# Weighing the 47-point groups three times as heavily in the table that paces spectral steps beside channel mixing

## The chip, the core and the metric

The kernel runs on one core of one Trainium2 chip. The metric is the device time of one execution in microseconds (us); lower is better. The time before is 2440.4 us, the median of three runs (2438.03 to 2441.76). On the core, TensorE (PE) does the matrix products, VectorE (DVE), ScalarE (ACT) and GpSimd (POOL) do elementwise work, and SyncE (SP) and ACT issue the transfers (DMA). Each engine works through its own queue in the order in which the program was built.

## The reference

Eight images of 3008 tokens by 256 channels go through two blocks in fp32.

```python
X = np.fft.rfft(x, axis=1)                       # along the tokens
Yr = Xr @ w_r - Xi @ w_i + b_r
Yi = Xr @ w_i + Xi @ w_r + b_i
Y  = soft-threshold of Yr and Yi by 0.01
x  = np.fft.irfft(Y, n=3008, axis=1)             # first block's output

h  = relu(x.transpose(0, 2, 1) @ w_tok1) @ w_tok2   # mixing over tokens
u  = x + h.transpose(0, 2, 1)
out = u + relu(u @ w_ch1) @ w_ch2                   # mixing over channels, 256 -> 1536 -> 256
```

## The kernel before, in words

**Units.** The images are worked in five units: image 0, image 1, and the pairs (2, 3), (4, 5) and (6, 7). They are called units 0 to 4 here. A product in near-fp32 accuracy is made of three matrix products of a high and a low part (helper `mm3`, lines 196 to 198), so one fp32 product shows as three rows.

**Spectral part of a unit** (generator `spectral`). Since 3008 = 47 x 64, the Fourier transform is done in two stages.

- *The 47-point groups* (`dft47`): 13 groups a unit, each of 5 values of the second index. For one group a tile `x` is loaded from memory three groups ahead, its sum and difference `sd` are formed (line 247 on POOL, line 248 on DVE; unit 1 has both on DVE), and split into a high part `xh` (ACT, line 146) and a low part `xl` (DVE, line 149). Six matrix products make the two results `p` (three for each). ACT copies them to a tile `a` (line 269), and ACT's queue then issues the store of `a` to the scratch tensor `a_d` (line 271). The tile `a` has two buffers.
- *The mixing steps*: 12 steps for each image of the unit. A step loads a slice of `a_d`, transforms it (64-point products `px`, line 469), copies it (`xf` by ACT, line 471), adds two of its parts (`xf` by POOL, line 472), splits it (`xth` on ACT, `xtl` on DVE), multiplies by the mixing weights (18 matrix products `pm`, lines 196 to 198), adds the bias and soft-thresholds on DVE (`z`, lines 498 and after), splits to `yh` and `yl`, and then does the first stage of the inverse transform (`pi`, copied to `bt` and stored to `b_d`) and the first token product (`gp`).

**Channel part of a unit** (generator `channel`). The unit's tokens are cut into chunks of up to 512. For each chunk the program forms the token mixing and the last stage of the inverse transform (`pu`), the first channel product (`ph`, six matrix products for each of 12 slices, rectified to `hh` on ACT and `hlo` on DVE), and the second (`po`, six for each slice). For units 2 to 4 the channel part runs after all spectral work is over, by Strassen's scheme (`channel7`).

**What sets the order.** The spectral parts of units 1 and 2 are woven between the channel slices of unit 0, and those of units 3 and 4 between the channel slices of unit 1 (table `BESIDE`). The last loop of `tile_kernel` does this with two budgets in estimated microseconds. `left_c` is the channel work still to come; every channel slice yields its estimate, which is taken off. `left_s` is the spectral work still to come; every spectral step yields its estimate, which is taken off in the same way. After each channel slice, spectral steps are written out until `left_s` is no more than `pace * left_c`, where `pace` was set to `left_s / left_c`. So a spectral step with a larger estimate is followed by more channel work. Where a generator yields "wait" (before a unit's first group where POOL forms `sd`, and after its last one), 10 us of channel work pass with no spectral step, and `pace` is set anew. A list scheduler then sees the written order and may move neighbouring instructions.

The estimate of a 47-point group is `0.7 * w / C`: 0.7 us for an image alone (w = 256, C = 256), 1.4 us for a pair. A mixing step's pieces yield 0.9, 2.15, 0.68 and 1.37 us per image. Over an image that sums to 13 x 0.7 + 12 x 5.1 = 70.3 us, the number in `left_s`.

Of the kernel before, what the change touches and what calls it, by code (L numbers as in the profile page):

```python
# [17 lines left out]
B, N, C = 8, 3008, 256  # L18
# [5 lines left out]
UNITS = [[0], [1]] + [[2 * p, 2 * p + 1] for p in range(1, NP)]  # L24
NG = 13
# [11 lines left out]
SEVEN = (2, 3, 4)  # L37
SPILL = (1, 2, 3, 4)
CW7 = 2 * CW
BESIDE = {0: [1, 2], 1: [3, 4]}  # L40


# [84 lines left out]
def tile_kernel(ctx: ExitStack, tc: tile.TileContext, io):  # L127
# [115 lines left out]
    def sum_diff(x, g, w, eng, pool):  # L243
        if eng is None:
            return x
        sd = t4([120, 2, w], "sd") if pool is None else wk.tile([120, 2, w], F32, tag=("xtl", "xf", "wt", "et")[g % 4], name="sd", bufs=2)
        eng.tensor_tensor(out=sd[:, 0], in0=x[:, 0], in1=x[:, 1], op=ALU.add)
        V.tensor_tensor(out=sd[:, 1], in0=x[:, 0], in1=x[:, 1], op=ALU.subtract)
        return sd

    def split_x(sd, w):
        xh, xl = hl([120, 2, w], "xh"), hl([120, 2, w], "xl")
        split(xh, xl, sd, S, V)
        return xh, xl

    def stage1(sd, dst, g, w, pool):
        n = GS if g < NG - 1 else N2 - GS * (NG - 1)
        a = ev([120, 2, w], "a") if pool is None else pool.tile([120, 2, w], F32, name="a", bufs=4)
        each = 512 // w
        for i0 in range(0, 2, each):  # L260
            pt = bank("p1")
            for i in range(i0, i0 + each):
                o = (i - i0) * w
                if pool is None:
                    mm3(pt[:, o:o + w], f1r[:, 0, i], f1r[:, 1, i], sd[0][:, i], sd[1][:, i], True, True)
                else:
                    PE.matmul(pt[:120, o:o + w], lhsT=f1[:, i], rhs=sd[:, 0], start=True, stop=False)
                    PE.matmul(pt[:120, o:o + w], lhsT=f1[:, 2 * i], rhs=sd[:, 1], start=False, stop=True)
            S.copy(out=a[:, i0:i0 + each].rearrange("p i w -> p (i w)"), in_=pt[:120])
        rows = dst.rearrange("(i n) k w -> (n k) i w", i=2)  # L270
        PUT.dma_start(out=rows[g * 120:g * 120 + n * KH, :, :w], in_=a[:n * KH])


    def stage1_turned(sd, z, g):
        n = GS if g < NG - 1 else N2 - GS * (NG - 1)
        pt = bank("p1")
        for t in range(2):
            for i in range(2):
                o = (2 * t + i) * GS * KH
                PE.matmul(pt[:, o:o + GS * KH], lhsT=sd[:, i, t * 128:(t + 1) * 128], rhs=f1[:, i], start=True, stop=True)  # L280
        S.copy(
            out=z.rearrange("p k (q n) -> p q k n", q=4)[:, :, :, g * GS:g * GS + n],
            in_=pt[:, :4 * GS * KH].rearrange("p (q n k) -> p q k n", q=4, n=GS)[:, :, :, :n],
        )

    def dft47(load, dst, w, ahead, eng, pool=None, turned=False):
        xs = [load(g) for g in range(ahead)]
        yield "wait" if eng is G else 0.0
        sds = {}

        def prepare(g):
            if g < NG:
                sds[g] = sum_diff(xs[g], g, w, eng, pool)
                xs[g] = None

        def divide(g):
            if g < NG and pool is None:
                sds[g] = split_x(sds[g], w)

        prepare(0)  # L300
        prepare(1)
        divide(0)
        for g in range(NG):
            if g + ahead < NG:
                xs.append(load(g + ahead))
            prepare(g + 2)
            divide(g + 1)
            if turned:
                stage1_turned(sds.pop(g), dst, g)
            else:  # L310
                stage1(sds.pop(g), dst, g, w, pool)
            yield 0.7 * w / C

    def f2cols(k1):
        j0 = (15 * k1) % N2
# [11 lines left out]
    def prepare_w1(pool, after):  # L327
        def load(g):
            f = load_wide(None, 2 * DT, pool, ("hl", "o")[g % 7 % 2], raw=raws.pop(g), after=after.get(g)).rearrange("p (i w) -> p i w", i=2)
            load_raw1()  # L330
            return f

        return dft47(load, a_w, DT, 2, None, pool)
# [222 lines left out]
    def spectral(u):  # L556
        p = parts(u)
        nb = p.nb
        yield from dft47(p.load_unit, p.a, p.w, 3, V if u == 1 else G)
        yield "wait"  # L560
        steps = [(kp, b) for kp in range(KP) for b in range(nb)]
# [42 lines left out]
    def begin(sp):  # L604
# [14 lines left out]
        with tc.tile_pool(name="early", bufs=1) as early:  # L619
# [3 lines left out]
            wc["fw"] = early.tile([128, 2, 128], F32, name="fw")  # L623
            z = wc["z"] = const.tile([128, KH, 2 * 128], F32, tag="w1", name="z")
            x = dft47(p.load_unit, z, p.w, NG, V, early, True)
            DMA.dma_start(out=wc["eye"], in_=io["eye"])
            next(x)
# [81 lines left out]
    for u, bs in enumerate(UNITS):  # L709
        total, at = N * len(bs), 0  # L710
        step = CW7 if u in SEVEN else CW
        widths = [k * TOKS for k in sizes] if u == 0 else [total % step] + [step] * (total // step)
# [47 lines left out]
    def make_u(g):  # L760
# [6 lines left out]
        for m in homes:  # L767
            if m not in ufs:
                ufs[m] = wc["uf"].tile([128, 2, CW7 if chunks[m][0] in SEVEN else CW], F32, name="uf", bufs=3)
        for ct in range(2):  # L770
# [230 lines left out]
    def channel7(ns):  # L1001
        channels.close()
        wc["tail"] = ctx.enter_context(tc.tile_pool(name="tail", bufs=1, reuse_waits="tile"))
        behind = None
        half = NF // 2
        for n in ns:
            after = n + 1 if n + 1 < len(chunks) else None
            mine = list(needs[after]) if after else []
            for p in range(half):
                hs = first7(n, p)  # L1010
                if behind:
                    second7(*behind, 0, (0, 1))
                if p < len(mine):
                    make_u(mine[p])
                    if p + 1 < len(mine):
                        load_wt2(mine[p + 1])
                        load_b2(mine[p + 1])
                if p == half - 2:
                    load_ahead(n + 2)
                if behind:  # L1020
                    second7(*behind, 1, (0, 1))
                    if p == 0:
                        for k in range(2):
                            finish7(behind[0], k, 2)
                behind = n, p, hs
                if after and p == half - 2:
                    sum_u(after)
                    for i in range(2):
                        split_u7(after, i)
                if after and p == half - 1:  # L1030
                    for i in range(2, 7):
                        split_u7(after, i)
        for k in range(2):
            for f in range(2):
                second7(*behind, f, (k,))
            finish7(behind[0], k, 2 - k)

    def run(gen):
        for _ in gen:
            pass  # L1040
# [3 lines left out]
    done = begin(sp)  # L1044
    for n, (u, at, cw) in enumerate(chunks):
        if u in SEVEN:
            channel7(range(n, len(chunks)))
            break
        if at == 0:
            if u:  # L1050
                sp, done = chain.from_iterable(spectral(v) for v in BESIDE[u]), 0.0
            else:
                sp = chain(sp, *(spectral(v) for v in BESIDE[u][1:]))
            left_s = sum(len(UNITS[v]) for v in BESIDE[u]) * 70.3 - done
            mine = [w for cu, _, w in chunks if cu == u]
            made = sum(k for gu, _, _, k in groups if gu == u) - sizes[0]
            left_c = 32.7 * (sum(mine) - mine[-1]) / CW + 3.6 * made * TOKS / GW + 0.5
            pace, hold = 0.0, left_c - (25.0 if u == 0 else 0.0)
        for c in channel(n):
            if c == "end":  # L1060
                run(sp)
                left_s = -1e9
                continue
            left_c -= c
            if hold is not None:
                if left_c > hold:
                    continue
                pace, hold = left_s / left_c, None
            while left_s > pace * left_c:
                step = next(sp, None)  # L1070
                if step is None:
                    left_s = -1e9
                elif step == "wait":
                    hold = left_c - 10.0
                    break
                else:
                    left_s -= step
# [36 lines left out]
```

## Time and profile before

| What | Value | Where it is from |
| --- | --- | --- |
| Median of three runs | 2440.4 us | times |
| The profiled execution's own time | 2437.33 us | times |
| Its span, first to last instruction | 2435.5 us | page, first line |
| PE busy | 2379.9 us (98% of the span) | page, part 1 |
| DVE, ACT, POOL busy | 1442.1, 1176.7, 309.1 us | page, part 1 |
| Mean granted TensorE clock | 0.994 | spans and clocks |
| Spectral parts of units 1 to 4 beside channel work | about 182 to 1130 us of the span | the tiles' first and last instructions |

The profile's busy shares are of one execution. A view by windows gives each engine's busy time in a stretch of the span, with PEclk, the share of its full speed that TensorE's clock was granted there, and the share of time that the 16 DMA engines worked. A view of waits names for an engine's idle time the instruction that ended it: "PE p L197 <- DVE xl L149" is idle time of PE before a product into `p` on line 197, ended by the DVE instruction on line 149 that writes `xl`. In a timeline, "[2.94 <-DMA a_d<-a]" behind a row means 2.94 us of idle time before it, ended by the landing of a store to `a_d`.

### The profile page before, as it was taken

What the parts mean: (1) busy time and instruction counts of PE and PEld (TensorE: products, weight loads), DVE (VectorE), ACT (ScalarE), POOL (GpSimd) and SP (SyncE); (2) the same over time, 40 slices, a digit from 0 to 9 for tenths busy, and PEclk for the clock granted to TensorE, in tenths of its full rate; (3) what the DMA queues carried; (4) which work ended last, traced back from release to release, by engine and by line L of the source; (5) the groups of instructions that cost most, each with busy time, mean ns of one, the idle gap of its engine ahead of it and who ended that gap; (6) DMA issues with size and microseconds to landing.
All of it is one profiled execution on the core that took longest, in us unless ns stands there. A gap on an engine that the chain in (4) does not pass through costs nothing.

```text
span 2435.5 us, 32450 instructions
## 1 busy us (share of the span) xinstructions
PE 2379.9 (98%) x12524; PEld 2063.7 (85%) x12524; DVE 1442.1 (59%) x2256; ACT 1176.7 (48%) x2105; POOL 309.1 (13%) x259
## 2 busy tenths in 40 slices
PE   8999999999999998999999999999999999999999
PEld 7778887989878886888988888898888889888887
DVE  7986666665455555655565555556555555555564
ACT  6764455444344445443454444444444544444443
POOL 0001333333123333331000000000000000000000
PEclk9999999999999999999999999999999999999999
DMA  8864465335453357333312102221211222122100
GB/s 215 250 211 140 137 192 177 123 122 168 136 164 105 104 155 214 104 113 100 95 59 66 61 21 77 66 80 59 66 61 36 62 66 80 59 66 63 53 2 35
DMA packets 146312, 253.48 MB, mean 104 GB/s; under 512 B 10549, under 2 KB 98701, under 8 KB 146157
## 3 DMA queue, kind: packets, MB, share of 16 engines
q1 hardware_dynamic: 115225, 194.24, 26.7%
q10 hardware_dynamic: 30932, 57.16, 7.1%
q8 instruction: 99, 1.62, 0.3%
q14 instruction: 56, 0.46, 0.1%
HBM read 163.41 MB, written 87.95 MB: 103 GB/s over the span
## 4 chain that ended last, share of the span: by engine, by line
PE 84%; DMA 6%; DVE 4%; ACT 3%; issue 2%; POOL 1%; SPq 1%; ACTq 0%; DVEq 0%; POOLq 0%
PE po L196 10%; PE po L198 10%; PE po L197 10%; PE pu L776 5%; DMA a_d<-a 3%; PE sx L196 3%; PE sx L198 3%; PE sx L197 3%; PE ph L196 2%; PE ph L197 2%; PE ph L198 2%; PE px L469 2%; PE sw L196 2%; PE sw L198 2%; PE sw L197 2%; PE pu L196 2%
## 5 line engine op out<-in xcount | busy, mean ns | idle before, releaser
L196 PE MATMUL po<-hh,w2h 128*128 128x512 f32 (+3 forms) x1176 | 453.0, 385 | 0.0
L197 PE MATMUL po<-hlo,w2h 128*128 128x512 f32 (+3 forms) x1176 | 449.5, 382 | 1.4 <-DVE hlo L815 1.4
L198 PE MATMUL po<-hh,w2l 128*128 128x512 f32 (+3 forms) x1176 | 448.7, 382 | 0.0
L944 ACT ACTIVATE hh<-sn 128x512 fp32r<-128x512 f32 (+1 forms) x432 | 270.8, 627 | 86.3 <-DVE sn L964 56.7
L945 DVE SCALAR_TENSOR_TENSOR hlo<-sn,hh 128x512 fp32r<-128x512 f32 (+1 forms) x432 | 290.3, 672 | 10.1 <-ACT hh L944 0.6
L197 PEld LDWEIGHTS po<-hlo,w2h 128*128 128x128 f32 x1176 | 220.9, 188 | 41.1 <-DVE hlo L815 4.5
L198 PEld LDWEIGHTS po<-hh,w2l 128*128 128x128 f32 x1176 | 220.8, 188 | 38.3
L196 PEld LDWEIGHTS po<-hh,w2h 128*128 128x128 f32 x1176 | 221.0, 188 | 37.8 <-ACT hh L814 1.4
L953 DVE TENSOR_TENSOR sn<-sq,sn 128x512 f32<-128x512 f32 (+1 forms) x108 | 73.4, 679 | 290.2 <-PE sq L198 267.0
L949 ACT COPY sn<-sx 128x512 f32<-128x512 f32 (+1 forms) x108 | 62.5, 579 | 341.7 <-PE sx L198 341.6
L815 DVE SCALAR_TENSOR_TENSOR hlo<-ph,hh 128x512 fp32r<-128x512 f32 (+3 forms) x156 | 98.9, 636 | 98.5 <-ACT hh L814 98.2
L196 PE MATMUL pm<-wmh,xth 128*128 128x256 f32 x504 | 148.0, 294 | 5.1 <-ACT xth L146 2.8
L198 PE MATMUL pm<-wmh,xtl 128*128 128x256 f32 x504 | 143.0, 285 | 3.0 <-DVE xtl L149 2.7
L197 PE MATMUL pm<-wml,xth 128*128 128x256 f32 x504 | 142.1, 282 | 0.0
L783 ACT COPY uf<-pu 128x470 f32<-128x470 f32 (+15 forms) x152 | 60.5, 426 | 167.8 <-PE pu L776 167.0
L149 DVE TENSOR_TENSOR xtl<-xf,xth 128x768 fp32r<-128x768 f32 x84 | 80.8, 962 | 100.2 <-ACT xth L146 100.2
L814 ACT ACTIVATE hh<-ph 128x512 fp32r<-128x512 f32 (+3 forms) x156 | 86.7, 556 | 105.3 <-PE ph L198 101.2
L776 PEld LDWEIGHTS pu<-g,b 96*128 96x128 f32 x1024 | 130.9, 191 | 3.4
L776 PE MATMUL pu<-g,b 96*128 96x94 f32 x1024 | 129.2, 271 | 0.0
L149 POOL TENSOR_TENSOR yl<-z,yh 128x512 fp32r<-128x512 f32 x72 | 97.0, 1347 | 220.1 <-ACT yh L146 212.8
L196 PE MATMUL ph<-uh,w 128*128 128x512 f32 (+3 forms) x312 | 120.5, 387 | 1.9 <-DVE z L498 1.0
L146 ACT CAST xth<-xf 128x768 fp32r<-128x768 f32 x84 | 70.1, 835 | 102.0 <-POOL xf L472 101.9
(185 smaller groups left out, 5395.3 us busy)
## 6 DMA issues: line engine op xcount, KB each, us to landing
wt<-wt_d SPq DMA_DIRECT2D x28, 940.0 KB, 5.8
x<-in_x SPq DMA_DIRECT2D x39, 480.0 KB, 5.1
a<-a_d SPq DMA_DIRECT2D x36, 512.0 KB, 3.8
b_d<-bt ACTq DMA_DIRECT2D x36, 512.0 KB, 3.3
a_d<-a ACTq DMA_DIRECT2D x36, 480.0 KB, 4.9
wt<-wt_d SPq DMA_DIRECT2D x21, 752.0 KB, 5.1
b<-b_d SPq DMA_DIRECT2D x32, 480.0 KB, 6.4
out<-uf SPq DMA_DIRECT2D x26, 512.0 KB, 4.5
```

What stands on the lines that cost most here:

```text
L146: S.copy(out=hi, in_=src)
L149: lo_eng.tensor_tensor(out=lo, in0=src, in1=hi.bitcast(F32), op=ALU.subtract)
L196: PE.matmul(out, lhsT=wh, rhs=xh, start=start, stop=False, skip_group_check=more)
L197: PE.matmul(out, lhsT=wh, rhs=xl, start=False, stop=False, skip_group_check=more)
L198: PE.matmul(out, lhsT=wl, rhs=xh, start=False, stop=stop, skip_group_check=more)
L776: PE.matmul(pt[:, s * TOKS:(s + 1) * TOKS], lhsT=b2[:, s, cs], rhs=g2[:, 0 if s0 + s == 0 else 1], start=False, stop=s == k - 1)
L814: S.activation(out=hh, in_=pt, func=AF.Relu)
L815: V.scalar_tensor_tensor(out=hlo, in0=pt, scalar=0.0, in1=hh.bitcast(F32), op0=ALU.max, op1=ALU.subtract)
L944: S.activation(out=hh, in_=t, func=AF.Relu)
L945: V.scalar_tensor_tensor(out=hlo, in0=t, scalar=0.0, in1=hh.bitcast(F32), op0=ALU.max, op1=ALU.subtract)
L949: S.copy(out=snap[0], in_=x)
L953: V.tensor_tensor(out=snap[0], in0=q, in1=snap[0], op=ALU.add)
```

## The change

A constant `SLOW = 2.1` takes the place of 0.7 in what a 47-point group yields, where the group runs beside channel work; the groups that run elsewhere (the weights' and unit 0's, which are given a pool) keep 0.7. The sum in `left_s` is raised by what that adds: 13 x 1.4 = 18.2 us an image, so 88.5 in place of 70.3. No product, copy or transfer is added or taken away. Units 2 to 4 keep Strassen's scheme (`SEVEN` is as it was).

```diff
@@ -37,6 +37,7 @@
 SEVEN = (2, 3, 4)
 SPILL = (1, 2, 3, 4)
 CW7 = 2 * CW
+SLOW = 2.1
 BESIDE = {0: [1, 2], 1: [3, 4]}
@@ -309,7 +310,7 @@
                 stage1_turned(sds.pop(g), dst, g)
             else:
                 stage1(sds.pop(g), dst, g, w, pool)
-            yield 0.7 * w / C
+            yield (SLOW if pool is None else 0.7) * w / C
@@ -1051,7 +1052,7 @@
                 sp, done = chain.from_iterable(spectral(v) for v in BESIDE[u]), 0.0
             else:
                 sp = chain(sp, *(spectral(v) for v in BESIDE[u][1:]))
-            left_s = sum(len(UNITS[v]) * 70.3 for v in BESIDE[u]) - done
+            left_s = sum(len(UNITS[v]) * (70.3 + NG * (SLOW - 0.7)) for v in BESIDE[u]) - done
```

The added line moves every later line number by one: line 269 before is line 270 after.

How this moves instructions is seen at two places. The first is ACT's queue at the first groups of unit 3 (images 4 and 5). `COPY a` moves a group's result out of `p` (two copies for a group, in two buffers `a`), `DMA a_d` issues its store, `CAST xh` splits the input of a later group, and `ACTIVATE hh` belongs to one channel slice. Before:

```order
L269 COPY a<-p_6251 120x512
L269 COPY a<-p_6256 120x512
L814 ACTIVATE hh<-ph 128x448
L271 DMA a_d_91<-a 120x2x512
L146 CAST xh<-sd 120x1024
L269 COPY a<-p_6289 120x512
L269 COPY a<-p_6294 120x512
L146 CAST xh<-sd 120x1024
L271 DMA a_d_91<-a 120x2x512
L269 COPY a<-p_6310 120x512
L269 COPY a<-p_6315 120x512
```

With the change, from the same group of the unit on:

```order
L270 COPY a<-p_6268 120x512
L270 COPY a<-p_6273 120x512
L815 ACTIVATE hh<-ph 128x448
L272 DMA a_d_91<-a 120x2x512
L147 CAST xh<-sd 120x1024
L270 COPY a<-p_6306 120x512
L270 COPY a<-p_6311 120x512
L815 ACTIVATE hh<-ph 128x448
L272 DMA a_d_91<-a 120x2x512
L147 CAST xh<-sd 120x1024
L270 COPY a<-p_6344 120x512
```

Before, groups follow each other with no channel slice between some of them; with the change a channel slice (`hh`) stands between each two of these groups. Over a unit, from the first product of its groups to the last, the PE rows of channel work (`ph`, `po`, and `pu` in brackets) go from 27 to 58 for the last ten groups of unit 1, from 60 to 124 (0 to 20) for unit 2, from 54 to 96 (22 and 22) for unit 3, and from 36 to 72 (0 to 20) for unit 4. Further on in unit 3 (the sixth to eighth group) three groups still stand with none between them.

The second place is PE's queue at an early mixing step of unit 3. `px` makes a step's 64-point products; the `pm` rows behind it are those of the step before it or of the step itself. Before:

```order
L197 MATMUL pm_6798<-wml,xth 128x256
L198 MATMUL pm_6798<-wmh,xtl 128x256
L469 MATMUL px<-f_78,a_6715 128x128 x4
L196 MATMUL ph<-uh,w_961 128x512
L197 MATMUL ph<-ul,w_961 128x512
L198 MATMUL ph<-uh,w_961 128x512
```

With the change, at the like step:

```order
L198 MATMUL pm_6866<-wml,xth 128x256
L199 MATMUL pm_6866<-wmh,xtl 128x256
L470 MATMUL px<-f_78,a_6783 128x128 x4
L197 MATMUL pm_6906<-wmh,xth 128x256
L198 MATMUL pm_6906<-wml,xth 128x256
L199 MATMUL pm_6906<-wmh,xtl 128x256
```

Before, a channel slice (`ph`, then `po`) stood between the `px` rows and the next step's `pm`; with the change it does not. Call a step bare if no more than the 18 `pm` products of another step and four `px` products stand between its `px` and its own `pm`. Leaving each unit's first step aside, 17 steps are bare with the change (1, 3, 4 and 9 in units 1 to 4) and 8 before (0, 0, 1 and 7). On every engine the number of instructions of each kind is the same in both programs.

More of the change, by code (lines that the diff above doesn't have):

```diff
@@ L1053, in tile_kernel @@
                 sp = chain(sp, *(spectral(v) for v in BESIDE[u][1:]))
-            left_s = sum(len(UNITS[v]) for v in BESIDE[u]) * 70.3 - done
+            left_s = sum(len(UNITS[v]) * (70.3 + NG * (SLOW - 0.7)) for v in BESIDE[u]) - done
             mine = [w for cu, _, w in chunks if cu == u]
```

## The prediction

> **What bounds the kernel now.** I read the page first, then busy time by windows, then the waits of the worst windows, then ACT's timeline there. The page:
>
> ```profile
> span 2435.5 us, 32450 instructions
> PE 2379.9 (98%) x12524; PEld 2063.7 (85%) x12524; DVE 1442.1 (59%) x2256; ACT 1176.7 (48%) x2105; POOL 309.1 (13%) x259
> ```
>
> TensorE (PE) is the bound, idle for 2435.5 - 2379.9 = 55.6 us in all. The change neither adds nor removes a product, so it can win only such idle time and time at a lowered clock. Where these lie shows when the span is cut at the 47-point groups of units 1 to 4 (rows 1, 3, 5 and 7) and the mixing steps behind each (rows 2, 4, 6 and 8); the last row is Strassen's part, which holds its place:
>
> ```profile
> core 0: us, PE busy (x) PEld busy (x) DVE busy (x) ACT busy (x) POOL busy (x), PEclk, DMA share, GB/s
> 180.00:208.00 28.00, 23.96 (x123) 20.63 (x123) 17.51 (x35) 14.43 (x27) 0.00 (x0) 0.88 0.64 187
> 208.00:348.00 140.00, 135.30 (x875) 125.41 (x874) 87.23 (x131) 63.90 (x116) 49.07 (x40) 0.99 0.46 138
> 348.00:388.00 40.00, 34.89 (x143) 25.34 (x142) 31.24 (x40) 27.31 (x44) 15.91 (x9) 1.00 0.80 249
> 388.00:652.00 264.00, 256.77 (x1583) 240.48 (x1581) 147.14 (x232) 112.01 (x203) 73.80 (x64) 0.99 0.41 126
> 652.00:690.00 38.00, 31.98 (x133) 24.19 (x133) 25.63 (x24) 23.31 (x38) 16.15 (x9) 0.96 0.83 249
> 690.00:911.00 221.00, 220.21 (x1295) 195.31 (x1294) 124.44 (x180) 98.36 (x170) 71.84 (x64) 1.00 0.41 126
> 911.00:949.00 38.00, 32.40 (x114) 21.56 (x113) 23.96 (x22) 24.16 (x38) 16.11 (x9) 0.91 0.78 230
> 949.00:1135.00 186.00, 182.05 (x1112) 162.14 (x1111) 108.30 (x158) 83.70 (x143) 63.48 (x58) 1.00 0.34 113
> 1135.00:2436.00 1301.00, 1296.09 (x6249) 1109.07 (x6247) 726.27 (x1127) 611.26 (x1116) 0.00 (x0) 1.00 0.20 60
> ```
>
> The four short stretches hold 144 us and PE's idle time in them is 4.0 + 5.1 + 6.0 + 5.6 = 20.7 us. The clock adds to that: a stretch of 28 us at a mean clock of 0.88 has lost 0.12 x 28 = 3.4 us. The others lost 0, 0.04 x 38 = 1.5 and 0.09 x 38 = 3.4 us. Together the units lose 7.4, 5.1, 7.5 and 9.0, that is 29.0 us. The mixing steps, 811 us long, have 4.7 + 7.2 + 0.8 + 4.0 = 16.7 us of idle time.
>
> What PE waits for in the groups of unit 4, by the waits of window 911 to 949 (us in total, times, longest):
>
> ```profile
> ACT a L269 <- DMA a_d<-a: 11.6, 5, 3.8
> DVE xl L149 <- ACT xh L146: 11.1, 9, 2.8
> ...
> PE p L197 <- DVE xl L149: 2.7, 4, 0.9
> PE p L196 <- ACT xh L146: 1.8, 2, 1.5
> ```
>
> Read from below: PE waits for xl and xh, DVE's xl waits for ACT's xh, and ACT stands still 11.6 us until stores to a_d land, because the copy into `a` has only two buffers and the next xh is queued behind that copy. ACT's timeline has it step by step:
>
> ```profile
> 923.01 1.07 ACT L269 COPY a<-p 120x512 f32<-120x512 f32 x2 [2.94 <-DMA a_d<-a]
> ...
> 930.44 1.07 ACT L269 COPY a<-p 120x512 f32<-120x512 f32 x2 [2.25 <-DMA a_d<-a]
> ...
> 938.14 1.07 ACT L269 COPY a<-p 120x512 f32<-120x512 f32 x2 [3.76 <-DMA a_d<-a]
> ```
>
> A buffer comes round after 923.01 to 930.44 to 938.14, 7.4 and 7.7 us for two groups. The stores' time to landing, first while the loads of x also run (917 to 935), then after the last of them (935 to 951):
>
> ```profile
> a_d<-a ACTq DMA_DIRECT2D x6, 480.0 KB, 6.1
> x<-in_x SPq DMA_DIRECT2D x5, 480.0 KB, 5.9
> ...
> a_d<-a ACTq DMA_DIRECT2D x4, 480.0 KB, 3.4
> ```
>
> So two buffers allow a pair of groups every 1.1 (the copies) + 6.1 = 7.2 us, 3.6 us a group, while x is loading, and 2.25 us a group afterwards.
>
> **The change part by part.**
>
> *More channel work between groups.* A row of 512 columns takes 0.23 us from start to start:
>
> ```profile
> 906.46 0.39 PE L196 MATMUL ph<-uh,w 128*128 128x512 f32 x1
> 906.69 0.39 PE L197 MATMUL ph<-ul,w 128*128 128x512 f32 x1
> ```
>
> For other widths I scale it by columns: 470 columns 0.21, 256 columns 0.115. A pair's 78 group products are 17.9 us of PE. With the counts of channel rows given with the change, and 0.11 us for a pu row of the last stage, PE needs a group (divided by the 12 intervals, 9 in unit 1):
>
> - unit 1: 60 x 0.115 + 27 x 0.21 = 12.6 us, 1.4 a group; with 58 rows 19.1 us, 2.1 a group;
> - unit 2: 17.9 + 60 x 0.21 = 30.5, 2.5; with 124 and 20 rows 46.1, 3.8;
> - unit 3: 17.9 + 54 x 0.21 + 22 x 0.11 = 31.7, 2.6; with 96 rows 40.5, 3.4;
> - unit 4: 17.9 + 36 x 0.23 = 26.2, 2.2; with 72 and 20 rows 36.7, 3.1.
>
> Against the stores' 3.6 us, unit 2 is now wide enough: of its 5.1 us I leave 1.0 for the one place where groups stand close. Unit 4 stays a little short of 3.6 for its first ten groups, about 9 x 0.5 = 4.5 us in arrears, which the quicker last stores cannot return; I leave 4.3 of 9.0. Unit 3 is wide enough in the mean but has three groups (sixth to eighth) without channel work between them: the third copy waits for the sixth group's store, 7.2 us against the 2 x 1.4 us in which PE gets there, 4.4 us; with the closer groups behind it I leave 5.0 of 7.5. In unit 1 (tiles of half the size) 12.6 us of work and 7.4 lost make 20.0 us over nine intervals, so the stores gave a group every 2.2 us; at 2.1 us of PE work this is about balanced, and I leave half, 3.7 of 7.4. Gain 4.1 + 4.7 + 2.5 + 3.7 = 15.0 us. Of this 3.4 is clock, a half of what units 1 and 4 lose by it. The bounds are 0 (the stores go on setting the pace) and 29.0 (all of it goes).
>
> A page of the Trainium skill speaks against the clock's part. "TensorE: Matmul & The Clock Gate" (Why this matters for your kernels) lets the clock fall to half only behind PE-idle gaps of about 3 us and more. By that rule gaps like these cost no clock, spacing gives none back, and the sum below would be 3.4 us smaller. The trace differs: in the window from 180 to 208 the clock fell to 0.88 with no single wait of PE over 1.3 us (the row for `p` L197 below). I go by the trace.
>
> ```profile
> PE p L197 <- DVE xl L149: 12.8, 17, 1.3
> PE p L196 <- ACT xh L146: 6.2, 7, 1.9
> ...
> PE pw L349 <- DMA aw<-a_w: 0.3, 1, 0.3
> ```
>
> *Less channel work between mixing steps.* A group's estimate triples, but a unit's share of the budget does not change, so the mixing steps must end where they did: they are 61.2 of 88.5 in place of 61.2 of 70.3, a fifth less channel work to each. What that uncovers is the chain from px to pm. Its pieces in the two last mixing stretches:
>
> ```profile
> L471 ACT COPY xf<-px x48: 577/587/591, 706.3 to 1112.4; 128x512 f32<-128x512 f32 x48
> L472 POOL TENSOR_TENSOR xf<-xf x48: 728/741/1400, 706.9 to 1113.4; 128x256 f32<-128x256 f32 x48
> L146 ACT CAST xth<-xf x48: 831/834/842, 707.7 to 1114.2; 128x768 fp32r<-128x768 f32 x48
> L149 DVE TENSOR_TENSOR xtl<-xf,xth x48: 944/959/1164, 708.6 to 1115.1; 128x768 fp32r<-128x768 f32 x48
> ```
>
> 0.59 + 0.74 + 0.83 + 0.96 = 3.1 us, while a bare step has 18 x 0.115 + 4 x 0.11 = 2.5 us of PE work to cover it. In unit 4 before, with 7 bare steps, the waits are these:
>
> ```profile
> PE pm L198 <- DVE xtl L149: 2.2, 5, 0.5
> PE pm L196 <- ACT xth L146: 1.4, 3, 0.6
> ```
>
> Eight waits cost 3.6 us, 0.45 each. Nine more bare steps (17 against 8) cost 9 x 0.45 = 4.1 us. From below the bound is 0: unit 3 before waited 0.8 us in all, and a step may be bare on PE's queue while its chain started early. From above every bare step costs 0.45 + 0.66 (the POOL sum at its longest, 1.40, in place of 0.74) + 0.59 (a channel hh ahead of xf on ACT) = 1.70 us, in all 17 x 1.70 - 3.6 = 25.3 us. I take 4.1, since the price was measured on just such steps.
>
> *What costs nothing.* With each group move its load of x on SP's queue, POOL's and DVE's sd, ACT's xh and a, and the store on ACT's queue. They keep their order among themselves; the loads of channel weights and of `b` queue behind x on SP as before. The cover is the lookahead of several channel slices: in the whole span PE waits for a landing only once, for 0.3 us (the pw row above). Were it gone, a late load of some 5.9 us would stand in the channel work, at most once a unit. The stores of a unit's last groups come later, but 10 us of channel work stand between them and the first px, against a landing of 3.4. The other waits of the mixing steps (pi, ph and others in units 1 and 2) may shift either way by some 3 us; I count 0.
>
> *Sum.* -15.0 + 4.1 = -10.9 us. On the profiled execution's 2437.3 us (span 2435.5 and 1.8 around it) that is 2426.4. The median of the runs shown lies 3.1 above that execution, so for a median I forecast 2440.4 - 10.9 = 2429.5 us.
>
> **The rivals.**
>
> *All of the stretches' loss goes.* With fewer groups in a microsecond, loads and stores meet less, stores land nearer 3.4 than 6.1 us, and two buffers allow a group every 2.3 to 3 us, quicker than PE asks for it. For it: the DMA share of 0.78 to 0.83 in the pairs' stretches. Against it: the three close groups in unit 3. -29.0 + 4.1 = -24.9, 2415.5 us.
>
> *Half of it.* The scheduler's order leaves clumps, and each clump fills both buffers again; units 1 and 3 gain nothing and the others a part. -7.5 + 4.1 = -3.4, 2437.0 us: no difference. For it: unit 3's order. Against it: unit 2's, where hardly a clump is left.
>
> *Slower.* The mixing steps become the bound: at each bare step ACT's queue holds an hh ahead of xf, and POOL's sum takes 1.40 us. This decides once a bare step costs more than (15.0 + 3.6) / 17 = 1.09 us, over twice the 0.45 measured. At 1.70 us each: -15.0 + 25.3 = +10.3, 2450.7 us. For it: the longest POOL sum. Against it: its median of 741 ns hardly differs from its shortest, 728. The Trainium skill has a ground for such long sums: "GPSIMD Engine Reference" (1. Specifications) has POOL share its SBUF interfaces with VectorE, and denser mixing overlaps the two more; the row's spread agrees.
>
> **How the numbers follow.** The forecast gets 0.57, all of the loss 0.15, half of it 0.18, slower 0.10. The forecast's own range is 2421 to 2438; to hold the time 8 times in 10 I go from 2414 (all of it gone) to 2443 (above the half, short of the slower case). A measurement of this kernel tells about 0.2% (4.9 us) from no change, so faster means under 2435.5: 0.15 + 0.51 of the forecast's + 0.04 of the half's = 0.70. Slower is over 2445.3: 0.08. That leaves 0.22 for no difference.
>
> **What would show it.** Right: ACT's wait for a_d (38.8 us in the row below) falls by more than half, PE's waits for xl and xh (12.8 and 6.2) to under half, and the clock holds 1.00 in the groups of units 2 and 4, while pm's waits for xth and xtl rise by some 4 us over units 1 to 4.
>
> ```profile
>   DMA a_d<-a: 38.8, 21
> ```
>
> Wrong: the groups stretch out but PE's idle time in them stays, so that the stores were not what held it; or pm's waits rise by over 10 us.

## The result, and the profile after

The changed kernel takes 2419.4 us (median of four runs, 2417.8 to 2422.0); the kernel before, run beside it, 2441.1 us (2438.0 to 2443.4). The ratio is 0.9913, 95% interval 0.9896 to 0.9930, so 21 us are won, 17 to 25 by the interval. Between the two profiled executions, which the traces below are of, it is 2437.33 - 2420.87 = 16.5 us. The page after:

```profile
span 2419.0 us, 32459 instructions
PE 2372.6 (98%) x12524; PEld 2064.8 (85%) x12524; DVE 1447.3 (60%) x2256; ACT 1175.8 (49%) x2105; POOL 308.9 (13%) x259
```

Busy time by windows of the changed kernel, cut like the prediction's: rows 1, 3, 5 and 7 are the 47-point groups of units 1 to 4, rows 2, 4, 6 and 8 the mixing steps behind them, the last row is Strassen's part. Columns after the engines' busy times are TensorE's granted clock, the DMA share and GB/s.

```profile
core 0: us, PE busy (x) PEld busy (x) DVE busy (x) ACT busy (x) POOL busy (x), PEclk, DMA share, GB/s
180.00:215.00 35.00, 31.66 (x171) 27.47 (x170) 24.60 (x48) 17.87 (x34) 0.00 (x0) 0.95 0.58 177
215.00:344.00 129.00, 125.30 (x836) 117.12 (x835) 85.95 (x120) 58.65 (x109) 50.76 (x40) 1.00 0.49 144
344.00:396.00 52.00, 49.99 (x228) 42.01 (x227) 36.78 (x47) 32.12 (x54) 14.37 (x9) 0.97 0.76 235
396.00:638.00 242.00, 238.19 (x1494) 224.25 (x1493) 142.14 (x223) 104.81 (x192) 72.36 (x64) 1.00 0.40 125
638.00:692.00 54.00, 49.16 (x210) 40.35 (x210) 31.46 (x31) 30.19 (x50) 16.44 (x9) 0.91 0.74 225
692.00:896.00 204.00, 202.33 (x1208) 179.92 (x1207) 118.15 (x172) 92.67 (x158) 72.61 (x64) 1.00 0.40 125
896.00:942.00 46.00, 45.04 (x200) 35.26 (x199) 29.27 (x29) 29.30 (x49) 16.18 (x9) 1.00 0.78 231
942.00:1119.00 177.00, 170.65 (x1046) 151.57 (x1045) 104.32 (x152) 80.43 (x135) 63.48 (x58) 1.00 0.33 110
1119.00:2419.00 1300.00, 1295.69 (x6248) 1108.91 (x6246) 725.88 (x1127) 610.91 (x1116) 0.00 (x0) 1.00 0.20 60
```

The stretches are longer, as written (unit 2's 52 us in place of 40), and three of the four hold less idle time of PE: 3.3, 2.0 and 1.0 us in units 1, 2 and 4 against 4.0, 5.1 and 5.6. Unit 3 had 6.0 us of idle time at a clock of 0.96 and now has 4.8 us at 0.91: nothing was won there. The last row is as it was.

PE's busy time itself fell by 7.3 us, with the same products. A part of that is the clock. Another is that a product's busy time (0.39 us for 512 columns) is longer than its distance to the next (0.23), so a wait of up to some 0.16 us hides inside it. From here on I therefore count **lost time**: from the start of each PE row to the start of the next, less the median distance of rows of that width, wherever that is over 0.04 us; it is put down to the row that came late, and a halved clock counts in it too. It is worked out from all PE rows of a trace. A unit runs from the last token result of the unit before to its own; its stretch from 2 us before its first copy into `a` to 1.5 us after its last.

| Lost time, us | Before | After |
| --- | --- | --- |
| group stretches of units 1, 2, 3, 4 | 8.4, 8.5, 10.7, 12.1 (39.6) | 6.6, 4.9, 10.7, 3.0 (25.2) |
| mixing steps, `pm` rows, units 1 to 4 | 2.4, 4.2, 3.1, 8.7 (18.3) | 1.8, 5.8, 4.9, 12.1 (24.5) |
| mixing steps, other rows, units 1 to 4 | 8.0, 9.3, 1.4, 0.6 (19.4) | 6.2, 3.0, 0.9, 0.3 (10.4) |
| length of units 1, 2, 3, 4 | 185.8, 266.5, 294.0, 234.2 | 181.5, 257.3, 295.0, 228.6 |

So the stretches won 14.4 us, pm rows lost 6.2, and other rows of the mixing steps won 9.0, which the prediction did not have. Unit 1 also began 1.7 us later. Who PE waited for, over the whole span of the changed kernel (us in total, times, longest), the rows for groups and mixing:

```profile
PE pm L199 <- DVE xtl L150: 6.1, 14, 0.5
...
PE p L197 <- ACT a L270: 4.0, 3, 2.1
PE p L198 <- DVE xl L150: 3.8, 6, 1.9
...
PE pm L197 <- ACT xth L147: 3.2, 7, 1.1
PE px L470 <- DMA a<-a_d: 2.8, 1, 2.8
...
PE p L197 <- ACT xh L147: 1.1, 2, 0.9
```

and the two pm rows of the kernel before:

```profile
PE pm L196 <- ACT xth L146: 2.8, 6, 0.7
PE pm L198 <- DVE xtl L149: 2.7, 6, 0.5
```

The groups' waits fell from 12.8 + 6.2 (and 0.5 for a copy into `a`) to 3.8 + 4.0 + 1.1 us; the mixing products' rose from 5.5 to 9.3. The `px` row is new: once, in unit 1, PE waited 2.8 us for a load from a_d. The stores, though, hardly got quicker, and in unit 2 they got slower. There the medians to landing were, first before (window 349 to 380), then with the change (window 348 to 380):

```profile
a_d<-a ACTq DMA_DIRECT2D x9, 480.0 KB, 5.2
x<-in_x SPq DMA_DIRECT2D x8, 480.0 KB, 5.9
```

```profile
a_d<-a ACTq DMA_DIRECT2D x8, 480.0 KB, 7.3
x<-in_x SPq DMA_DIRECT2D x8, 480.0 KB, 6.4
```

Over the whole stretches of units 3 and 4 (windows 650 to 692 and 910 to 950 before, 638 to 692 and 896 to 942 with the change) the stores' median went from 5.0 to 4.6 and from 4.3 to 4.1 us.

ACT still waited 29.8 us for stores to a_d, against 38.8; less of that reaches PE, which has channel work in the meantime. Why unit 3 won nothing shows on ACT at its sixth to eighth group:

```profile
661.53 0.37 ACTq L272 DMA_DIRECT2D a_d<-a  x1
...
662.56 0.32 ACTq L272 DMA_DIRECT2D a_d<-a  x1
669.28 1.07 ACT L270 COPY a<-p 120x512 f32<-120x512 f32 x2 [5.81 <-DMA a_d<-a]
670.24 0.56 ACT L815 ACTIVATE hh<-ph 128x448 fp32r<-128x448 f32 x1
670.39 0.32 ACTq L272 DMA_DIRECT2D a_d<-a  x1
```

Two stores leave 1 us apart, both buffers are taken, and the third group's copy stands 5.81 us, with the next hh and xh behind it.

### The profile page after: what moved, and what is told of

It is laid out like the page before. It is cut to its first block, busy times and chain, and to the rows that moved or that the text cites. A ratio compares the mean times of both kernels' runs of the same rounds, so it can differ in the third digit from the quotient of the medians.

```text
span 2419.0 us, 32459 instructions
## 1 busy us (share of the span) xinstructions
PE 2372.6 (98%) x12524; PEld 2064.8 (85%) x12524; DVE 1447.3 (60%) x2256; ACT 1175.8 (49%) x2105; POOL 308.9 (13%) x259
## 4 chain that ended last, share of the span: by engine, by line
PE 77%; DVE 3%; ACT 2%; DMA 2%; POOL 2%; issue 2%; DVEq 0%; SPq 0%; ACTq 0%; POOLq 0%
PE po L197 10%; PE po L198 10%; PE po L199 10%; PE pu L777 4%; PE sx L197 3%; PE sx L198 3%; PE sx L199 3%; PE sw L197 2%; PE sw L198 2%; PE sw L199 2%; PE ph L197 2%; PE ph L199 2%; PE ph L198 2%; PE pu L197 2%; PE pu L198 2%
## 5 line engine op out<-in xcount | busy, mean ns | idle before, releaser
L946 DVE SCALAR_TENSOR_TENSOR hlo<-sn,hh 128x512 fp32r<-128x512 f32 (+1 forms) x432 | 290.2, 672 | 10.1 <-ACT hh L945 0.6
```

Of the source, the lines that this page charges most:

```text
L946: V.scalar_tensor_tensor(out=hlo, in0=t, scalar=0.0, in1=hh.bitcast(F32), op0=ALU.max, op1=ALU.subtract)
```

## The experiments

Theory 1 is the prediction's: two buffers of `a`, each held until its store has landed, set the pace where groups stand close. Rival 2 is that each group's split on ACT and DVE is what is too slow for close groups.

**Four buffers of `a`, in the kernel before and in the changed one.** In both the same edit:

```diff
-        a = ev([120, 2, w], "a") if pool is None else ...
+        if pool is None:
+            a = wk.tile([120, 2, w], F32, tag="ev" if g % 4 < 2 else "wt", name="a", bufs=2)
```

> The kernel before, with the tile `a` of a 47-point group beside channel work given four buffers in place of two (two of them those of `wt`, which no group needs). The order of the matrix products stays that of the kernel before. Lost time is counted from start to start of PE's rows against the usual distance of such a row; in the group stretches the kernel before loses 8.8, 8.2, 10.4 and 11.9 us, 39.3 in all. Theory 1 (two buffers of `a`, each held until its store lands, set the groups' pace): ACT's wait for a_d, 38.8 us before, falls under 10, the stretches lose 15 to 25 us in place of 39.3, and the time falls by 14 to 24 us. Rival 2 (the close order itself is at fault: each group's split into xh and xl takes ACT and DVE longer than PE's products do, whatever the buffers): the a_d wait goes, but waits for xh and xl stay, and the time moves by under 4 us. Rival 3 (the DMA engines are full there, so stores and loads only change places): a_d's wait goes, waits for the loads of x come in its place, under 6 us won.

Measured: 2425.9 us (2423.2 to 2431.4) beside 2439.7; ratio 0.9944 (0.9931 to 0.9958), 13.7 us. The stretches lose 7.8, 6.7, 5.3 and 6.6, 26.5 us in place of 39.6; pm and other rows stay (18.0 and 18.8). ACT's waits for a_d are gone. What is left, of the waits from 140 to 1200 us:

```profile
PE p L197 <- DVE xl L149: 15.6, 17, 1.8
POOL sd L247 <- DMA x<-in_x: 9.2, 3, 5.2
...
PE p L196 <- ACT xh L146: 2.2, 2, 1.3
```

Both theories hold a part. The stores' share is 13.1 us of 39.6. Behind it PE waits for xl as often as before (17 times, 15.6 us): with the order as close as this, VectorE's split is late next. POOL's wait for loads of x was already 8.6 us before, so those waits did not take the stores' place, as rival 3 had it. The gain is just short of what theory 1 asked for.

> The changed kernel with the same four buffers of `a`. It loses 6.6, 4.6, 10.4 and 3.1 us in the group stretches of units 1 to 4, most in unit 3, where three groups stand close. Theory 1: unit 3's stretch loses under 5 us in place of 10.4 and the others a little less, in all 8 to 12 us less than the changed kernel, that is 29 to 33 us under the kernel before. Rival 2 (close order at fault): unit 3's stretch still loses 8 to 10 us and the time is that of the changed kernel within 3 us.

Measured: 2410.5 us (2408.8 to 2412.3) beside 2439.7; ratio 0.9878 (0.9862 to 0.9893): 29.2 us under the kernel before, and 9 under the changed kernel. The stretches lose 5.8, 0.9, 6.7 and 1.1, 14.4 us in place of 25.2. This beats both kernels. Unit 2 went from 4.9 to 0.9, unit 1 only from 6.6 to 5.8. Unit 3 went from 10.7 to 6.7, not under 5, so something beside the stores is left there.

**What are the other rows' 9 us?** Most of them are pi rows of unit 2. Before, PE waited there (window 388 to 652):

```profile
PE pi L196 <- ACT bt L523: 2.8, 1, 2.8
PE pi L196 <- DVE hlo L815: 1.7, 1, 1.7
PE pm L196 <- DVE hlo L815: 0.8, 1, 0.8
```

ACT stood for raw token weights near two of these places. So the loads were left out first, in both kernels:

```diff
+        if fill:
+            V.memset(raw.rearrange("p n w -> p (n w)").bitcast(F32), 0.0)
+        else:
             DMA.dma_start(out=raw..., in_=src.bitcast(U32))
...
-            wfs[g] = [load_wide(io["wt2"][0, jt][:, cols], k * TOKS, pool) for jt in range(2)]
+            srcs = [io["wt2"][0, jt][:, cols] for jt in range(2)]
+            wfs[g] = [load_wide(src, k * TOKS, pool, raw=load_raw(src, k * TOKS, pool, g > 0)) for src in srcs]
```

> The kernel before, with the loads of the raw second token weights for groups 1 to 6 of unit 0 left out and their tiles filled with zeros by VectorE, so the token mixing of those tokens is not computed; the narrowing behind it stays. This takes away what ACT's narrowing waits for (11.8 us of ACT's idle time in units 1 and 2 before, 9.1 in the changed kernel). Theory 4 (the rest of the change's gain, some 9 us at pi, ph and gp in the mixing of units 1 and 2, came from these ACT waits falling at other places of the order): the kernel before gains 8 to 12 us from it. Rival 5 (those waits come from elsewhere, or vary from run to run): under 3 us.

> The changed kernel with the same loads left out (token mixing of groups 1 to 6 of unit 0 not computed). Theory 4: it gains 2 to 5 us from it, less than the kernel before does, so between these two kernels without raw loads the change is worth 13 to 17 us in place of some 19. Rival 5: it gains nothing, and the change is worth as much as with the loads.

Measured: from the kernel before 2429.2 us beside 2439.7, ratio 0.9956 (0.9944 to 0.9968), 10.5 us won; from the changed kernel 2422.0, ratio to the kernel before 0.9920 (0.9907 to 0.9933), which wins nothing over its 2419.4. The times look like theory 4, the traces do not: the other rows lose 18.4 us without the loads against 19.4 with them, and the pi rows of unit 2 still 4.6 of 5.8. What fell in the first is unit 1's stretch (8.4 to 4.5) and pm (18.3 to 15.3). Theory 4 is not borne out; why leaving out the loads helps the one kernel and not the other stays open (VectorE's fills with zeros are new work in both).

What stood at the waits that stayed is VectorE's narrowing of these weights, 12 instructions in one burst. The end of one in the kernel before, VectorE's timeline with two of the burst's rows and what waits among them:

```profile
517.91 0.68 DVE L506 TENSOR_TENSOR z<-z 128x512 f32<-128x512 f32 x1
518.51 1.08 DVE L167 SCALAR_TENSOR_TENSOR wide<-wide 128x376 uint32<-128x376 uint32 x1
...
520.77 1.61 DVE L167 SCALAR_TENSOR_TENSOR wide<-wide 128x376 uint32<-128x376 uint32 x1
...
523.03 0.94 DVE L149 TENSOR_TENSOR xtl<-xf,xth 128x768 fp32r<-128x768 f32 x1
```

and ACT in the same stretch, where the copy out of `pi` stands behind a cast that waits for the burst:

```profile
522.88 0.51 ACT L146 CAST wt<-wide 128x376 fp32r<-128x376 f32 x1 [1.91 <-DVE wide L170]
523.29 0.58 ACT L523 COPY bt<-pi 128x512 f32<-128x512 f32 x1
```

PE's 2.8 us wait for bt ended there. In the kernel before, the bursts from unit 1 on begin at 199.7, 280.5, 348.5, 427.8 and 514.9 us, three of them amid mixing steps. With the change they begin at 198.4, 273.3, 347.6, 402.7 and 488.8: that at 402.7 falls into the 10 us of channel work behind unit 2's groups. To test this, the narrowing itself was left out, in both kernels:

```diff
-            wfs[g] = [load_wide(io["wt2"][0, jt][:, cols], k * TOKS, pool) for jt in range(2)]
+            if g == 0:
+                wfs[g] = [load_wide(...) for jt in range(2)]
+            else:
+                wfs[g] = [wk.tile([128, 2, k * TOKS], F32, tag="o", name="wide", bufs=3)[:, 0] for _ in range(2)]
+                for wf in wfs[g]:
+                    V.memset(wf, 0.0)
```

> The kernel before, with the loads and the whole narrowing of the second token weights for groups 1 to 6 of unit 0 left out: each tile is filled with zeros by one VectorE instruction in place of six on VectorE and two on ScalarE, so the token mixing of those tokens is not computed. Leaving out the loads alone did not take the waits away at pi and ph in the mixing of units 1 and 2 (19.4 us lost there at other rows than pm, 18.4 without the loads). The narrowing comes in bursts of 12 VectorE instructions (8.9, 8.0 and 6.9 us of work at 280, 428 and 515 us of the span), just where PE waits. Theory 6 (the bursts hold up z, hlo and the copies behind them, and the change won some 9 us because one burst fell behind a group stretch, where it is covered): these other losses of units 1 and 2 fall from 17.3 to under 8 us, and the time by 10 to 18 us. Rival 7 (the waits come from the mixing steps themselves): the other losses stay above 13 us and the time falls by under 5 us.

> The changed kernel with the same narrowing left out (token mixing of groups 1 to 6 of unit 0 not computed). Theory 6: it gains 4 to 9 us, less than the kernel before does, so without the bursts the change is worth 6 to 13 us: what its group stretches win (14.4) less what its pm rows lose (6.2), 8.2 us. Rival 7: it gains under 3 us, and the change is worth some 19 us as with the bursts.

Measured: the kernel before 2423.4 us (2421.5 to 2432.0) beside 2440.0, ratio 0.9940 (0.9921 to 0.9959), 16.6 us won; the changed kernel 2402.7 us (2400.6 to 2410.2), ratio to the kernel before 0.9854 (0.9836 to 0.9871), 16.7 us under its own time (14 by the two ratios). In unit 2 the theory holds. PE's waits there in the kernel before without narrowing (window 385 to 645):

```profile
PE p L197 <- DVE xl L149: 1.3, 1, 1.3
PE pm L196 <- ACT xth L146: 0.7, 1, 0.7
```

The pi rows' long waits are gone: unit 2's other rows lose 1.9 us in place of 9.3, and in the changed kernel 1.1 in place of 3.0. So of the 6.3 us that the change won at these rows of unit 2, all but 0.8 goes with the bursts. In unit 1 the sum of other rows did not fall (9.7 in place of 8.0), but this profiled execution (2432.0, 8.6 above its median) lost some 7 us of that at pu and ph rows of the unit's start, where the clock stood at half from 153 to 167 us. Behind unit 1's groups the other rows lost 2.5 us in place of 6.3, and in the changed kernel 1.7 in place of 4.3, its 2.8 us wait of `px` among what went.

The second half of theory 6 fell: the changed kernel gains some 14 to 17 us, where 4 to 9 were expected, and the change is worth 20.7 us without the bursts. Its gain comes at another place. Busy time of the changed kernel without narrowing, in the group stretches of units 1 and 2:

```profile
172.00:193.00 21.00, 21.00 (x122) 19.19 (x121) 12.18 (x23) 8.39 (x16) 0.00 (x0) 1.00 0.40 110
332.00:383.00 51.00, 51.00 (x244) 44.34 (x243) 32.17 (x39) 32.32 (x53) 15.67 (x9) 1.00 0.72 214
```

PE is busy throughout, at full clock: these stretches lose 0.1 and 0.3 us, in place of 6.6 and 4.9. What the change had left there differs by unit. PE's longest waits with the change were these, first unit 1 (window 186 to 215), then unit 2 (window 344 to 396):

```profile
PE po L198 <- DVE hlo L816: 1.8, 1, 1.8
PE ph L197 <- DVE hlo L816: 0.9, 1, 0.9
```

```profile
PE p L197 <- ACT a L270: 1.7, 1, 1.7
```

In unit 1 both `hlo` stand among the burst that began at 198.4, and four buffers hardly helped: that is the burst. In unit 2 the burst of 347.6 was over at 354.3, and PE's wait, at 378.6, was for a copy into `a` that had waited 3.29 us for a store: that is the stores still, and four buffers alone took it away (0.9 us). Leaving out narrowing took it away too, as ACT's wait for a_d in that stretch fell from 9.0 to 1.6 us; whether by the missing loads or by the order is not shown. Without narrowing the change takes the four stretches from 38.6 to 11.1 us.

**One group behind a channel slice.** The close groups of unit 3, tried with two buffers, with four, and with four beside unit 1's channel work alone (there `if u == 1 and step == 2 * SLOW`):

```diff
                     left_s -= step
+                    if step in (SLOW, 2 * SLOW):
+                        break
```

> The changed kernel, in which the pacing loop leaves off behind each 47-point group beside channel work, so that no two groups follow one channel slice (the scheduler may still put two side by side: one place in each of units 2, 3 and 4). Two buffers of `a`, as in the changed kernel. Theory 1 (stores set the pace where groups stand close): unit 3's stretch, which loses 10.7 us with three close groups, loses 3 to 5 us, unit 2's 3 to 5 in place of 4.9 and unit 1's 3 to 6 in place of 6.6; with 19 bare mixing steps in place of 17 the pm rows lose 1 us more; in all 5 to 10 us under the changed kernel. Rival 8 (unit 3's stretch loses for another reason than the close groups): it keeps over 8 us, and the time is that of the changed kernel within 3 us.

> The same with four buffers of `a`. Theory 1: with the groups spaced, the stores have little left to hold, so four buffers win 2 to 5 us more than one group a slice alone, and the stretches lose 8 to 12 us in all; the time is 2404 to 2412 us beside a kernel before at 2440. Rival 2 (VectorE's split of close groups is the rest): the same, since spacing answers to that too; it would show in waits for xl below 3 us in all. If four buffers win over 6 us more here, spacing did not free the stores.

Measured: 2421.3 us beside 2440.0 with two buffers, ratio 0.9920 (0.9906 to 0.9934), and 2417.3 with four, ratio 0.9908 (0.9895 to 0.9922). The stretches do as theory 1 says: with two buffers they lose 1.1, 2.5, 4.8 and 1.6, 10.1 us in place of 25.2, unit 3 less than half of its 10.7. With four it is 7.5 us, so four buffers win little more once groups are spaced. But the time does not follow: it is no better than the changed kernel's. In unit 1, which takes 195.5 us in place of 181.5, other rows lose 19.7 us in place of 6.2. The longest of it on ACT:

```profile
332.27 0.54 ACT L163 ACTIVATE raw<-raw 128x376 f32<-128x376 uint32 x1 [4.79 <-DMA raw<-in_wt]
...
333.61 0.42 ACT L147 CAST et<-ef 128x256 fp32r<-128x256 f32 x1
```

The split `et` stands behind a copy that waits for a load, and PE waits 4.2 us for `et`. Here a raw load does cost PE time.

> The changed kernel with four buffers of `a`, and the pacing loop leaving off behind each 47-point group only beside unit 1's channel work, so in units 3 and 4; units 1 and 2 stand in the order of the changed kernel, since there the one-group rule cost 13 us at other rows. Theory 1: unit 3's stretch loses 2.5 us, as with both edits, in place of the 6.7 us with four buffers alone, the pm rows stay (17 bare steps in both), and the time is 3 to 5 us under that of four buffers alone (2410.5), 2405 to 2408 us beside a kernel before at 2440. Rival 8 (the close groups are not what unit 3 loses by): 2409 to 2412 us.

Measured: 2410.6 us beside 2437.5, ratio 0.9887 (0.9874 to 0.9901), no better than four buffers alone. Unit 3's stretch lost the forecast 2.5 us in place of 6.7, and its length fell from 292.0 to 289.9: the close groups are what it had lost by. But pm and other rows lost 1.3 and 1.4 us more, and unit 1 began 1.7 us later, so it is given back.

**Other weights, with four buffers.** `SLOW = 3.5` and `SLOW = 1.4` in place of 2.1:

> The changed kernel with four buffers of `a` and 3.5 in place of 2.1 for SLOW: groups wider still, mixing steps closer, 21 bare steps in place of 17. If spacing and bareness trade as in the change (6.2 us of pm rows for 9 more bare steps, 0.7 each), pm rows lose 3 us more than the 26.5 of four buffers alone, and the stretches, at 14.4 us, lose 3 to 8 us less: 2406 to 2412 us, no better than 2 % of what the change won. If bareness costs more than the price measured, over 2414 us.

> The same with 1.4 for SLOW: half of the change's step, 16 bare steps, groups of the pairs 2.6 to 3.9 us of PE work apart in unit 2 and often 1.4 to 2.8 in units 3 and 4. Theory 1 with VectorE's split as its second part: the stretches lose 16 to 22 us (26.5 with 0.7 and four buffers, 14.4 with 2.1), pm rows 22 to 25, so 2412 to 2420 us, between the two. If the four buffers alone are what spacing stood for, it is within 3 us of 2.1 with four buffers (2410.5).

Measured beside 2437.5: 2416.3 us for 3.5, ratio 0.9911 (0.9898 to 0.9925); 2420.2 us for 1.4, ratio 0.9928 (0.9915 to 0.9941). Both are slower than 2.1 with four buffers.

| Four buffers of `a`, lost time in us | SLOW as 0.7 (before) | 1.4 | 2.1 | 3.5 |
| --- | --- | --- | --- | --- |
| group stretches | 26.5 | 18.9 | 14.4 | 4.8 |
| pm rows (bare steps) | 18.0 (8) | 21.7 (16) | 26.5 (17) | 28.8 (21) |
| other rows | 18.8 | 18.2 | 9.7 | 19.8 |
| time, us | 2425.9 | 2420.2 | 2410.5 | 2416.3 |

The stretches fall and pm rows rise with the weight, and their sum is lowest at 3.5, the largest weight tried. What makes 2.1 the best of the four is the third row, which follows no such order. At 3.5 its longest waits are single ones in unit 1 (3.7 us for `hlo`, 2.2 for `et`). That they too come of where the narrowing and the loads fall is likely after the runs above, but was not tested at these weights. At 3.5 the stretches' gain was larger than expected (9.6 us), pm's loss smaller (2.3), and 10.1 us at other rows ended it.

## Why the prediction was right, and where not

**The result lies in the range, at twice the forecast's gain.** Forecast was 10.9 us, measured 21 (17 to 25), or 16.5 between the profiled executions. It is below the forecast's own range (2421 to 2438) and inside the wide one, which had been drawn for another case, the one in which all the loss goes; that it held is in part luck. All of it lies where it was looked for, beside channel work; Strassen's part is unchanged.

**The mechanism of the stretches was right; it was a part of the cause.** Stores to a_d with two buffers did hold the close groups: four buffers alone won 13.7 us. The step "the stores set the pace" took them for the whole: with four buffers 26.5 of 39.6 us stayed, most of the waits for VectorE's split. Spacing answers to both, buffers to the stores alone; the burst in unit 1 answers to neither.

**The stretches' gain, -15.0 us, came out at 14.4**, and so near by luck, for its terms miss in both directions: unit 1 won 1.8 (forecast 3.7), unit 2 3.6 (4.1), unit 3 nothing (2.5), unit 4 9.1 (4.7). In unit 4 the copies were taken to be 4.5 us in arrears; the trace has it losing 3.0 in all. In unit 1 the rest was put down to the stores, and was a burst of narrowing. The clock's 3.4 us within the gain came out at nothing (below). The base was too small as well: idle time and clock gave 29.0 us, from start to start it is 39.6, since the waits' first part hides in the products' busy time.

**Bare steps, +4.1 us, came out at 6.2.** The count held and the price was low: 6.2 for nine more steps is 0.69 each, not 0.45. The 0.45 was idle time, 3.6 us in unit 4 before; from start to start the pm rows there lost 8.7 us. The cover was misread as well: the trace before has 192 `px` rows for unit 4's 24 steps, eight a step and not four, and five of the eight bare steps take 3.08 us from the last `px` to their own `pm`, not 2.5. Cover and chain (3.1 us) are about equal, which fits so small a price. The slower rival stayed away: the bare steps added 6.2 us, and it needed more than 15.0. Its long POOL sums are still the exception (720, 739 and 1402 ns with the change).

**The term that failed is "I count 0"** for the other waits of the mixing steps, some 3 us either way. It was -9.0 us. In unit 2 it is shown: 6.3 us by the profile, of which 5.5 go with the narrowing. Behind unit 1's groups 2.0 us were won, and 0.8 without narrowing; the rest is not settled. That the change moves a burst of other work was no term of the prediction, so this part of the gain is luck. The late load under "what costs nothing" did come, once: 2.8 us before `px`.

**The rival in which all goes** argued that stores land sooner once the groups are spaced. They landed later in unit 2 (7.3 against 5.2 us) and hardly sooner in units 3 and 4, where 0.4 and 0.2 us went; the gain came without it.

**The clock.** The prediction weighed a rule of the Trainium skill, "TensorE: Matmul & The Clock Gate" (Why this matters for your kernels), by which PE's idle gaps between matmuls should stay under some 3 us if the clock is to hold, against a trace in which shorter ones brought it down. The trace after is on the same side: 0.91 in unit 3's stretch, where PE's longest single waits were 2.1 us (for a) and 1.9 us (for xl), and 1.00 in unit 4's stretch, whose waits went. But the 3.4 us that spacing was to give back did not come: by the times at which each trace lists a new clock, both kernels ran 17.1 us at half clock in the four stretches, 10.2 us less in units 1 and 4 and 10.2 more in units 2 and 3. The 6.8 us at half clock in the mixing steps before are gone. Of the signs named beforehand, PE's waits and the rise of pm's (3.8 us of idle time against some 4) came as said; ACT's wait for a_d fell by a quarter, not by half, and unit 2's clock was 0.97, not 1.00.

## What to carry to other kernels

Where one queue fills its buffers faster than their stores land, a second kind of work between them hides the waits without making the stores faster; more buffers do it too, and the two together did better (29 us) than either (21 and 14). When steps are moved by a pacing table, count what the other, rare work of the stretch will meet at its new place: here bursts of narrowing that no part of the change touched were worth some 5 us in one unit by where they fell. Count loss from start to start, not by idle time: a quarter of it stood in busy time here (39.6 against 29.0 us).

## What was not expected of the hardware

In unit 2, stores of 480 KB took longer to land with the groups wider apart (median 7.3 us against 5.2), although the DMA share was lower (0.76 against 0.80 in the unit's stretches). Why is not shown; in units 3 and 4 they did not.

In the kernel before and with the change, TensorE's clock was halved behind single waits of 1.2 to 2.3 us, none of them near 3. One fall in unit 1 of the kernel before:

```profile
core 0: us, PE busy (x) PEld busy (x) DVE busy (x) ACT busy (x) POOL busy (x), PEclk, DMA share, GB/s
197.40:200.81 3.41, 1.24 (x6) 0.84 (x6) 2.38 (x7) 2.15 (x5) 0.00 (x0) 1.00 0.97 273
200.81:207.64 6.83, 5.95 (x20) 5.47 (x21) 4.25 (x9) 3.12 (x6) 0.00 (x0) 0.50 0.50 163
```

and one in unit 3 with the change:

```profile
666.62:670.04 3.42, 1.32 (x7) 0.82 (x6) 0.68 (x1) 0.76 (x2) 1.78 (x1) 1.00 0.98 359
670.04:673.45 3.41, 3.41 (x9) 2.72 (x10) 0.62 (x1) 3.21 (x6) 0.00 (x0) 0.50 0.65 175
```

The windows are cut at the clock's own steps: the falls of a trace lie whole multiples of 3.41 us apart. Between 150 and 1200 us the 13 traces of this case have 48 falls. In the 3.41 us ahead of each, PE was idle for 1.37 us or more in all, and no stretch of that grid with over 1.76 us idle went without a fall. Ahead of the first fall above it was 2.17 us, with no single wait over 1.3. So idle time adds up within such a stretch, and the limit is near half of it. This is read from the traces, whose ends of matmuls are modelled; no run varied the idle time alone.
